# A head in written order on all engines, product stores on the SP queue, later block loads

## The chip, the cores and the metric

The kernel runs on one core of one Trainium2 chip. The metric is the device time of one launch in microseconds (us).

## The reference

Eight batches of 576 tokens, eight heads of 64. The computation is in float32:

```
scores = q k^T / 8;  ret = scores * D     # D[h,i,j] = gamma_h^(i-j) for i >= j, else 0
x  = (ret v)   as [4608 tokens, 512]
h  = ((x w1) * (x w2)) w3                 # w1, w2: 512 x 1024, w3: 1024 x 1024
y  = h w_out                              # 1024 x 512
u  = y w2_in                              # 512 x 2048
out = (u - tanh(u)) w2_out                # 2048 x 512
```

The weights come in as float64.

## The kernel before, in words

**Precision.** Each large product is made of three matmuls (`mm3`, lines 116 to 121: high x high, low x high, high x low). A float64 block of a weight ("raw", 512 KB) is turned into a high and a low part by a `Conv` job (lines 123 to 169): `load` is a DMA on the SP queue, `a` and `c` are one ACT instruction each (lines 141, 158), `b` is four DVE instructions (lines 146 to 149), `d` two (lines 164, 165). A `Queue` runs a job in two steps: step one is `b` of this job and the load of a later one, step two is `a` of the next job and `c`, `d`, `e` of this one.

**Attention.** A batch is five chunks of 128 tokens (the last has 64), 40 chunks in all. For each chunk: `attn_load` (three DMAs on SP, line 223; scaling of q on DVE, line 227, and of v by eight ACT instructions, line 215), `attn_1` (transposes of q and k on PE, line 238, copied out by ACT, line 242), `attn_2` (scores on PE, line 255, masked by two DVE instructions into `pt`, line 257), `attn_3` (product with the running state, line 353, with v, line 359, the update of the state, lines 367 to 377, and the result split into the high and low part of the token tile `x`, ACT line 384 and DVE line 385). Batches 0 and 1 (chunks 0 to 9, the "head") go this way. From chunk 10 on, "the third batch" and those behind it, q and k come in small block loads instead (`load_qk`, 32 DMAs per pair of chunks, put in the list `pend` and issued on SP by `trickle`, line 291, at most ten per unit), k and v by `load_kv` (line 307), POOL scales q (`stage_q`) and DVE transposes both (`stage_0`, lines 338 and 340).

**Units.** 12 token tiles of 384 by 8 column blocks are 96 units. A unit is two halves (`half_s`, 12 matmuls each, line 119 to 121, into PSUM tile `psab`), then ACT copies the first half out (`a`, line 412) and DVE multiplies it with the second (`pf`, line 417). The product goes to DRAM (`pdr`), from where the next stage loads it (`p_load`, line 646). Its store is issued on the ACT queue in the unit behind (list `late`, line 415). Tile `tp` has two buffers.

**Order.** In the prologue and in units 0 to 9 only PE's order is the written one (`manual_schedule(engines={PE})`, line 512); the other engines and queues are ordered by the planner. From unit 10 (`NAUTO`, line 554) all engines follow the written order. `conv_at` (line 545) says how many steps of the w1/w2 conversion stand in front of unit n; `chunk_at` says at which unit a chunk's `attn_3` stands. From unit 16 `side_s` runs the conversions of w_out and w3 (95 steps over the remaining units), the product w3 w_out, and at the end those of half of w2_out. A stage of chunk i has its unit in `stages` (line 550). A DMA handed to `later` is issued by `tick` some units on.

Of the kernel before, what the change touches and what calls it, by code (L numbers as in the profile page):

```python
# [8 lines left out]
F32 = mybir.dt.float32  # L9
# [19 lines left out]
def retention_glu_tanh_kernel(  # L29
# [16 lines left out]
    PE, ACT, DVE, POOL, SP = nc.tensor, nc.scalar, nc.vector, nc.gpsimd, nc.sync  # L46
# [3 lines left out]
    P = 128  # L50
# [3 lines left out]
    CH = [(s, min(C, S - s)) for s in range(0, S, C)]  # L54
    NA = len(CH)
    KD = DM // P
    FF = w1.shape[1] // P
    FF2 = w2_in.shape[1] // P
    T = 384
# [9 lines left out]
    pdr = [dram.tile([P, FF, T], F32, name=f"pdr{i}") for i in range(NTL)]  # L69
# [20 lines left out]

    sl_ = ExitStack()
    xp = sl_.enter_context(tc.tile_pool(name="xp", bufs=3, reuse_waits="tile"))
    tp = sl_.enter_context(tc.tile_pool(name="tp", bufs=2, reuse_waits="tile"))
# [9 lines left out]
    def later(eng, o, i_, n):  # L105

        held.append([n, eng, o, i_])

    def tick():
        for e in held:  # L110
            e[0] -= 1
        while held and held[0][0] <= 0:
            _, eng, o, i_ = held.pop(0)
            eng.dma_start(out=o, in_=i_)
# [88 lines left out]
    A = {}  # L203
# [13 lines left out]
    def attn_load(i):  # L217
        b, c = chunks[i]
        s0, n = CH[c]
        ts = []  # L220
        for nm, src in zip("qkv", qsrc):
            t = sap.tile([P, H, D], F32, name=f"{nm}n", bufs=4)
            SP.dma_start(out=t[:n], in_=src[b, s0:s0 + n])
            ts.append(t)
        A[i] = ts
        qn, kn, vn = ts
        DVE.tensor_tensor(qn[:n], qn[:n], dec_q[:n, c, :].unsqueeze(2).to_broadcast([n, H, D]), op=ALU.mult)
        scale_act(vn, dec_v, n, c)

    def attn_1(i):  # L230
        b, c = chunks[i]
        s0, n = CH[c]
        qn, kn, vn = A[i]
        tr = []
        for nm, src in (("q", qn), ("k", kn)):
            ps = psa.tile([P, NP, C], F32, tag="a", name=f"ps{nm}")
            for j in range(NP):
                PE.transpose(
                    ps[:, j, :n], src[:n, 2 * j:2 * j + 2, :].rearrange("p h d -> p (h d)"), ident[:n, :n]
                )  # L240
            t = sap.tile([P, NP, C], F32, name=f"{nm}T")
            ACT.activation(t[:, :, :n], ps[:, :, :n], AF.Copy)
            tr.append(t)
        A[i] = (kn, vn, tr[0], tr[1])
# [100 lines left out]
    def attn_3(i):  # L345
        b, c = chunks[i]
        s0, n = CH[c]
        kn, vn, qT, pt = A.pop(i)
        po = psa.tile([P, NP, C], F32, tag="a", name="pso")
        if c > 0:  # L350
            for j in range(NP):
                for e in range(2):
                    PE.matmul(  # L353
                        po[D * e:D * e + D, j, :n], state[:, j, D * e:D * e + D], qT[:, j, :n],
                        start=(j == 0), stop=False, skip_group_check=True,
                    )
        for j in range(NP):
            for e in range(2):
                PE.matmul(  # L359
                    po[D * e:D * e + D, j, :n], vn[:n, 2 * j + e, :], pt[:n, j, e, :n],  # L360
                    start=(c == 0 and j == 0), stop=(j == NP - 1), skip_group_check=True,
                )
        if c + 1 < NA:
            pu = psa.tile([P, NP, D], F32, tag="a", name="psu")
            for j in range(NP):
                for e in range(2):
                    PE.matmul(
                        pu[D * e:D * e + D, j, :], kn[:n, 2 * j + e, :], vn[:n, 2 * j + e, :],
                        start=True, stop=True,
                    )  # L370
            for e in range(2):
                sl = slice(D * e, D * e + D)
                st = state[sl, :, sl]
                if c == 0:
                    DVE.tensor_copy(st, pu[sl])
                else:
                    DVE.tensor_tensor(st, pu[sl], st, op=ALU.add)
        t0 = b * S + s0
        while t0 < b * S + s0 + n:
            ti = t0 // T  # L380
            m = min((ti + 1) * T, b * S + s0 + n) - t0
            x = xtile(ti)
            a0, o0 = t0 - b * S - s0, t0 - ti * T
            ACT.activation(x[:, 0, :, o0:o0 + m], po[:, :, a0:a0 + m], AF.Copy)
            DVE.tensor_tensor(  # L385
                x[:, 1, :, o0:o0 + m], po[:, :, a0:a0 + m], x[:, 0, :, o0:o0 + m].bitcast(F32), op=ALU.subtract
            )
            t0 += m


    ws = {}
    late = []

    def half_s(t, m, i):
        x = xt[t]
        w = ws[m]
        ps = psm.tile([P, 512], F32, tag="m", name="psab")
        for kk in range(KD):
            o = i * 1024 + kk * P
            mm3(  # L400
                ps[:, :T], (w[:, o:o + P], w[:, o + 512:o + 512 + P]), (x[:, 0, kk, :], x[:, 1, kk, :]),
                kk == 0, kk == KD - 1,
            )
        return ps

    def unit_s(t, m, mid=None):
        pss = [half_s(t, m, 0)]
        if mid is not None:
            mid()
        pss.append(half_s(t, m, 1))  # L410
        a = tp.tile([P, T], F32, name="a")
        ACT.activation(a, pss[0][:, :T], AF.Copy)  # L412
        while late:
            o, i_ = late.pop()
            ACT.dma_start(out=o, in_=i_)
        pf = tp.tile([P, T], F32, name="pf")
        DVE.tensor_tensor(pf, a, pss[1][:, :T], op=ALU.mult)  # L417
        late.append((pdr[t][:, m], pf))
        if m == FF - 1:
            del xt[t]  # L420

# [86 lines left out]
            yield  # L508


    ordered = ExitStack()
    ordered.enter_context(tc.manual_schedule(engines={mybir.EngineType.PE}))
    NH = 2 * NA
    for c in range(3):
        attn_load(c)
        q12.jobs[c].load()
    attn_load(3)
    attn_1(0)
    attn_1(1)
    attn_2(0, sap)  # L520
    q12.step()
    q12.step()
    attn_3(0)
    attn_load(4)
    attn_2(1, sap)
    attn_1(2)
    q12.step()
    attn_3(1)
    attn_load(5)
    attn_2(2, sap)  # L530
    attn_1(3)
    q12.step()
    attn_3(2)
    attn_load(6)
    attn_2(3, sap)


    units = [
        (0, 0), (0, 1), (0, 2), (0, 3), (0, 4), (1, 0), (1, 1), (1, 2),
# [2 lines left out]
    N0 = len(units)  # L542
    units += [(t, m) for t in range(2, NTL) for m in range(FF)]

    conv_at = [5, 9, 13, 17, 20, 21, 22, 23, 25, 27, 29, 31, 32]

    chunk_at = {0: 2, 1: 3, 2: 4, 3: 5, 4: 6, 6: 7, 8: 8, 10: 9}
    stages = []
    for i in range(NH, len(chunks)):
        p = int(13.0 + 2.3 * (i - NH))  # L550
        stages += [(p - 1, stage_q, (i,)), (p, stage_0, (i,)), (p + 1, stage_1, (i,)), (p + 2, attn_3, (i,))]
    stages.sort(key=lambda e: e[0])

    NAUTO = 10
    TRK = 10
    SIDE = 95
    sn = 0
# [3 lines left out]
    w34_ = ExitStack()  # L561
    w34 = []
    for n, (t, m) in enumerate(units):
        if n == NAUTO:
            ordered.close()
            ctx.enter_context(tc.manual_schedule())
        if n < len(conv_at):
            while q12.n < conv_at[n]:
                q12.step()
        if n == N0:  # L570
            assert not q12.step()
            sa_.close()
            cv = cv_.enter_context(tc.tile_pool(name="conv", bufs=2, side="right", reuse_waits="tile"))
            wg = wg_.enter_context(tc.tile_pool(name="wg", bufs=2, side="right", reuse_waits="tile"))
            for f in range(FF):
                wo[f] = wg.tile([P, 1024], F32R, name=f"wo{f}", bufs=1)
            side = side_s()
        while side is not None and sn < (n - N0 + 1) * SIDE / (len(units) - N0 - 1):
            sn += 1
            if next(side, 1) == 1:  # L580
                side = None
        tick()
        trickle(TRK)
        i = chunk_at.get(n)
        if i is not None and i > 2:
            attn_3(i)
            if i + 4 < NH:
                attn_load(i + 4)
            if i + 1 < NH:
                attn_2(i + 1, sap)  # L590
        unit_s(t, m, (lambda: attn_1(i + 2)) if i is not None and i + 2 < NH else None)
        if n == 5:
            load_qk(NH)
            load_kv(NH)
        if n == 8:
            load_qk(next_pair(NH))
        while si < len(stages) and stages[si][0] <= n:
            stages[si][1](*stages[si][2])
            si += 1
    assert si == len(stages) and not pend and not held and len(w34) == FF, (si, len(pend), held)  # L600
    assert side is None or next(side, None) is None
    for o, i_ in late:
        ACT.dma_start(out=o, in_=i_)
    sl_.close()
    lp_.close()

# [244 lines left out]
```

## Time and profile before

| | |
|---|---|
| runs, median of 3 | 1669.49 us (1668.22 to 1792.84) |
| the profiled execution's own time | 1668.11 us |
| its span | 1666.3 us |
| PE busy | 1607.6 us, 96% |
| DVE, ACT, POOL busy | 67%, 53%, 2% |
| mean granted clock of TensorE | 0.992 of 2.4 GHz |

The span runs from the first to the last instruction; 1.8 us of the execution's own time lie outside it. Busy shares are means over stages with different limits: in the first two of the page's 40 slices PE is busy for 5 tenths, in nearly all others for 9 tenths or more. "SPq" and "ACTq" in a row are DMA issues on those queues; a matmul's row shows a span that overlaps with the next one's, so the pace of matmuls is read from one start to the next.

### The profile page before, as it was taken

The page shows a single profiled execution, that of the slowest core. Times are in us where ns is not written, and L with a number is a line of the kernel's source. Part 1 is how long each engine was busy: PE and PEld are TensorE (multiplying, and loading weights), DVE is VectorE, ACT ScalarE, POOL GpSimd, SP SyncE. Part 2 cuts the span into 40 slices and gives each one's busy share as a digit, 9 for nine tenths or more (in the row PEclk, how much of TensorE's full clock was granted, in tenths as well). Part 3 has the DMA queues.
Part 4 walks back from the last instruction along what each step waited for, and adds up shares of the span by engine and source line. Part 5 has one row for each costly group of instructions (what it writes and reads, how often), then busy time and mean ns, then how long its engine had stood idle before and what let it go on. Part 6 is the DMA issues. An engine that isn't in the chain of part 4 may idle for free.

```text
span 1666.3 us, 26840 instructions
## 1 busy us (share of the span) xinstructions
PE 1607.6 (96%) x10128; PEld 1492.9 (90%) x10128; DVE 1118.6 (67%) x2006; ACT 876.4 (53%) x1929; POOL 31.1 (2%) x35
## 2 busy tenths in 40 slices
PE   5599989999999999999999999999999999999999
PEld 4489979989899999999999999999999999999997
DVE  6484655545454455676758788787887887778776
ACT  5352333323233232444447777777777777777775
POOL 0000000000001000000000000000000000000000
PEclk9799999999999999999999999999999999999999
DMA  8831565555546465766641001000100010001000
GB/s 195 193 105 66 132 149 131 143 126 141 114 117 141 109 254 191 218 203 221 198 188 45 20 20 38 20 20 19 39 19 20 20 38 20 20 19 39 1 19 20
DMA packets 261250, 157.96 MB, mean 95 GB/s; under 512 B 209152, under 2 KB 238080, under 8 KB 261120
## 3 DMA queue, kind: packets, MB, share of 16 engines
q1 hardware_dynamic: 245568, 127.93, 28.6%
q10 hardware_dynamic: 15552, 28.32, 4.5%
q8 instruction: 79, 1.29, 0.3%
q14 instruction: 51, 0.42, 0.1%
HBM read 110.05 MB, written 46.14 MB: 94 GB/s over the span
## 4 chain that ended last, share of the span: by engine, by line
PE 88%; SPq 4%; DMA 3%; DVE 2%; ACT 1%; issue 1%; ACTq 0%; DVEq 0%
PE psh L121 8%; PE psh L119 8%; PE psh L120 8%; PE psout L121 8%; PE psout L119 8%; PE psout L120 8%; PE psab L119 7%; PE psab L121 7%; PE psab L120 7%; PE psy L121 4%; PE psy L119 4%; PE psy L120 4%; SPq L291 3%; PE pss L255 2%; PE pso L359 1%; PE pso L353 1%
## 5 line engine op out<-in xcount | busy, mean ns | idle before, releaser
L119 PE MATMUL psab<-x,w 128*128 128x384 f32 x768 | 266.0, 346 | 0.0
L121 PE MATMUL psab<-x,w 128*128 128x384 f32 x768 | 259.0, 337 | 1.2 <-DVE x L385 1.2
L121 PE MATMUL psh<-yhl,w2i 128*128 128x384 f32 x768 | 258.9, 337 | 0.0
L120 PE MATMUL psab<-x,w 128*128 128x384 f32 x768 | 258.6, 337 | 0.0
L119 PE MATMUL psh<-yhl,w2i 128*128 128x384 f32 x768 | 258.1, 336 | 0.0
L120 PE MATMUL psh<-yhl,w2i 128*128 128x384 f32 x768 | 257.9, 336 | 0.0
L121 PE MATMUL psout<-w2o,g 128*128 128x512 f32 x576 | 227.0, 394 | 0.0
L119 PE MATMUL psout<-w2o,g 128*128 128x512 f32 x576 | 226.8, 394 | 0.0
L120 PE MATMUL psout<-w2o,g 128*128 128x512 f32 x576 | 225.4, 391 | 0.0
L740 ACT ACTIVATE u<-psh 128x384 f32<-128x384 f32 x192 | 94.4, 492 | 222.3 <-PE psh L121 222.1
L748 DVE TENSOR_TENSOR w<-u,psh 128x384 f32<-128x384 f32 x192 | 106.0, 552 | 80.7 <-ACT th L742 80.5
L761 DVE TENSOR_TENSOR g<-w,g 128x384 fp32r<-128x384 f32 x192 | 107.0, 557 | 69.9 <-ACT g L760 69.8
L120 PEld LDWEIGHTS psh<-yhl,w2i 128*128 128x128 f32 x768 | 144.2, 188 | 8.5
L119 PEld LDWEIGHTS psh<-yhl,w2i 128*128 128x128 f32 x768 | 144.3, 188 | 8.1
L119 PEld LDWEIGHTS psab<-x,w 128*128 128x128 f32 x768 | 145.7, 190 | 5.1
L417 DVE TENSOR_TENSOR pf<-a,psab 128x384 f32<-128x384 f32 x96 | 53.0, 552 | 140.4 <-PE psab L121 89.6
L121 PEld LDWEIGHTS psab<-x,w 128*128 128x128 f32 x768 | 145.3, 189 | 1.5 <-DVE x L385 1.5
L120 PEld LDWEIGHTS psab<-x,w 128*128 128x128 f32 x768 | 145.8, 190 | 0.5
L121 PEld LDWEIGHTS psh<-yhl,w2i 128*128 128x128 f32 x768 | 144.2, 188 | 0.0
L121 PEld LDWEIGHTS psout<-w2o,g 128*128 128x128 f32 x576 | 108.1, 188 | 25.6
L412 ACT ACTIVATE a<-psab 128x384 f32<-128x384 f32 x96 | 46.9, 488 | 159.4 <-PE psab L121 141.0
L119 PE MATMUL psy<-p,w 128*128 128x384 f32 x384 | 128.4, 334 | 1.9 <-ACT p L651 1.9
(85 smaller groups left out, 2901.5 us busy)
## 6 DMA issues: line engine op xcount, KB each, us to landing
pdr<-pf ACTq DMA_DIRECT2D x96, 192.0 KB, 2.3
pin<-pdr SPq DMA_DIRECT2D x48, 384.0 KB, 4.1
raw<-in_moe_w_dram SPq DMA_DIRECT2D x32, 512.0 KB, 5.4
raw<-in_moe_w_out_dram SPq DMA_DIRECT2D x24, 512.0 KB, 4.1
ydr<-ys ACTq DMA_DIRECT2D x12, 768.0 KB, 5.7
yin<-ydr SPq DMA_DIRECT2D x12, 768.0 KB, 4.2
out_dram<-os SPq DMA_DIRECT2D x36, 256.0 KB, 2.3
kn<-in_k_dram SPq DMA_DIRECT2D x32, 256.0 KB, 3.3
```

What stands on the lines that cost most here:

```text
L119: PE.matmul(ps, lh, rh, start=first, stop=False)
L120: PE.matmul(ps, ll, rh, start=False, stop=False)
L121: PE.matmul(ps, lh, rl, start=False, stop=last)
L255: PE.matmul(pss[e][:n, j, :n], kT[r:r + D, j, :n], qT[r:r + D, j, :n], start=True, stop=True)
L291: SP.dma_start(out=o, in_=i_)
L353: PE.matmul(po[D * e:D * e + D, j, :n], state[:, j, D * e:D * e + D], qT[:, j, :n], start=(j == 0), stop=False, skip_group_check=True,)
L359: PE.matmul(po[D * e:D * e + D, j, :n], vn[:n, 2 * j + e, :], pt[:n, j, e, :n], start=(c == 0 and j == 0), stop=(j == NP - 1), skip_group_ ...
L412: ACT.activation(a, pss[0][:, :T], AF.Copy)
L417: DVE.tensor_tensor(pf, a, pss[1][:, :T], op=ALU.mult)
L740: ACT.activation(u, h, AF.Square)
L748: DVE.tensor_tensor(w, u, h, op=ALU.mult)
L761: DVE.tensor_tensor(g[:, 1, :], w, g[:, 0, :].bitcast(F32), op=ALU.subtract)
```

## The change

All engines follow the written order from the beginning. In the prologue and in units 0 to 10 the instructions are written in a new order: loads of chunks 0 and 1 ahead of the first weight block, the scalings of q and v apart from the loads (`attn_scale`), the split into x apart from the rest of `attn_3` (`attn_x`), each ahead of the conversion steps that stand beside it. In a unit, `finish` (the copy `a`, the product `pf`) now stands behind the first half of the unit after; its store goes to the SP queue by `later(SP, ..., 1)`, issued at the start of the unit after that, ahead of the block loads of that unit; `pf` has three buffers. The conversion steps stand between the halves of the unit before the one that needs them. The first block loads of the third batch are put in the list after units 10 and 13 (before: 5 and 8), and the stages of its chunks start one unit later. After the last unit `finish` and `tick` issue the last two stores on SP.

```diff
+    ctx.enter_context(tc.manual_schedule())
...
+    def attn_scale(i):
...
+    def attn_x(i):
...
-    def unit_s(t, m, mid=None):
-        pss = [half_s(t, m, 0)]
-        if mid is not None:
-            mid()
-        pss.append(half_s(t, m, 1))
+    def finish():
+
+        if not open_:
+            return
+        t, m, pss = open_.pop()
         a = tp.tile([P, T], F32, name="a")
         ACT.activation(a, pss[0][:, :T], AF.Copy)
-        while late:
-            o, i_ = late.pop()
-            ACT.dma_start(out=o, in_=i_)
-        pf = tp.tile([P, T], F32, name="pf")
+        pf = tp.tile([P, T], F32, name="pf", bufs=3)
         DVE.tensor_tensor(pf, a, pss[1][:, :T], op=ALU.mult)
-        late.append((pdr[t][:, m], pf))
+        later(SP, pdr[t][:, m], pf, 1)
...
-    for c in range(3):
-        attn_load(c)
-        q12.jobs[c].load()
+    attn_load(0)
+    attn_load(1)
+    q12.jobs[0].load()
+    attn_load(2)
+    q12.jobs[1].load()
     attn_load(3)
+    q12.jobs[2].load()
+    attn_scale(0)
     attn_1(0)
+    attn_scale(1)
+    attn_2(0, sap)
     attn_1(1)
-    attn_2(0, sap)
     q12.step()
-    q12.step()
+    attn_scale(2)
     attn_3(0)
+    attn_x(0)
     attn_load(4)
     attn_2(1, sap)
+    q12.step()
     attn_1(2)
-    q12.step()
     attn_3(1)
     attn_load(5)
+    q12.step()
     attn_2(2, sap)
+    attn_x(1)
+    attn_scale(3)
     attn_1(3)
     q12.step()
     attn_3(2)
+    attn_x(2)
     attn_load(6)
     attn_2(3, sap)
+    attn_scale(4)
...
-    conv_at = [5, 9, 13, 17, 20, 21, 22, 23, 25, 27, 29, 31, 32]
+    conv_at = [8, 12, 16, 20, 21, 22, 23, 25, 27, 29, 31, 32]
...
-        p = int(13.0 + 2.3 * (i - NH))
+        p = int(14.0 + 2.28 * (i - NH))
...
-        unit_s(t, m, (lambda: attn_1(i + 2)) if i is not None and i + 2 < NH else None)
-        if n == 5:
+            if i + 2 < NH:
+                attn_scale(i + 2)
+        want = conv_at[n] if n < len(conv_at) else 0
+        pss = [half_s(t, m, 0)]
+        finish()
+        if want:
+            while q12.n < (want + q12.n) // 2:
+                q12.step()
+        if i is not None and i + 2 < NH:
+            attn_1(i + 2)
+        while q12.n < want:
+            q12.step()
+        pss.append(half_s(t, m, 1))
+        open_.append((t, m, pss))
+        if n == 10:
             load_qk(NH)
             load_kv(NH)
-        if n == 8:
+        if n == 13:
             load_qk(next_pair(NH))
...
-    for o, i_ in late:
-        ACT.dma_start(out=o, in_=i_)
+    finish()
+    tick()
```

## Rows read from the trace of the kernel before

**Rows 1.** Busy time by stage: window, length, each engine's busy time, clock, DMA share

```profile
0.00:110.00 110.00, 69.85 (x700) 62.10 (x701) 70.62 (x133) 52.65 (x141) 4.86 (x9) 0.92 0.80 183
...
200.00:240.00 40.00, 33.31 (x250) 31.04 (x250) 24.96 (x45) 13.77 (x41) 4.93 (x4) 0.91 0.59 138
240.00:560.00 320.00, 314.58 (x2567) 292.07 (x2566) 161.36 (x292) 97.06 (x271) 20.66 (x21) 0.99 0.53 129
```

**Rows 2.** PE's waits from 0 to 110: what waited for what: total, times, longest

```profile
PE psk L238 <- DVE x L385: 15.4, 2, 14.6
```

**Rows 3.** Timeline of DVE and ACT: start, length, instruction, idle time before

```profile
49.82 0.55 DVE L417 TENSOR_TENSOR pf<-a,psab 128x384 f32<-128x384 f32 x1
...
66.92 0.34 ACTq L415 DMA_DIRECT2D pdr<-pf  x1
67.31 0.60 ACT L384 ACTIVATE x<-pso 128x512 fp32r<-128x512 f32 x1 [18.34 <-DMA qb<-in_q_dram]
```

**Rows 4.** Chain that ended last, from 0 to 260: start, length, step

```profile
62.65 4.20 DMA qb<-in_q_dram
```

**Rows 5.** Timeline of SP, its first and last run of early block loads

```profile
23.92 3.68 SPq L291 DMA_DIRECT2D qb<-in_q_dram  x4
...
76.87 2.59 SPq L291 DMA_DIRECT2D kb<-in_k_dram  x5
```

**Rows 6.** Start of the head: busy time by window, then DVE's first instruction

```profile
0.00:20.00 20.00, 7.40 (x42) 6.11 (x44) 8.57 (x15) 11.20 (x32) 0.73 (x5) 1.00 1.02 224
...
5.26 0.69 DVE L227 TENSOR_TENSOR qn<-qn,dec 128x512 f32<-128x512 f32 x1 [5.26 <-DMA qn<-in_q_dram]
```

**Rows 7.** Timeline of PE: transposes; unit 5; attn_3 of chunk 7; unit 6

```profile
87.19 0.63 PE L238 MATMUL psq<-cst,qn 128*128 128x128 f32 x4
...
101.50 0.33 PE L119 MATMUL psab<-x,w 128*128 128x384 f32 x1
...
105.76 1.09 PE L353 MATMUL pso<-qT,state 128*64 128x128 f32 x16
...
109.21 0.44 PE L119 MATMUL psab<-x,w 128*128 128x384 f32 x1
```

**Rows 8.** Timeline of DVE: attention, then one conversion job

```profile
108.79 0.85 DVE L377 TENSOR_TENSOR state<-psu,state 64x256 f32<-64x256 f32 x2
...
111.47 1.28 DVE L257 TENSOR_TENSOR pt<-pss,cst 128x512 f32<-128x512 f32 x2
112.67 0.42 DVE L148 TENSOR_SCALAR ct<-cf 128x512 uint32<-128x512 uint32 x1
...
115.06 0.42 DVE L146 TENSOR_SCALAR ct<-raw 128x512 uint32<-128x512 uint32 x1
```

**Rows 9.** PE's waits from 110 to 700, the longest

```profile
PE pso L359 <- ACT vn L215: 6.3, 1, 6.3
```

**Rows 10.** Timeline ahead of that wait: SP's weight loads, and ACT behind them

```profile
206.87 0.39 SPq L135 DMA_DIRECT2D raw<-in_moe_w_out_dram  x1
...
219.38 0.38 SPq L135 DMA_DIRECT2D raw<-in_moe_w_out_dram  x1
...
223.49 0.66 ACT L141 ACTIVATE cf<-raw 128x512 f32<-128x512 f32 x1 [10.88 <-DMA raw<-in_moe_w_out_dram]
```

**Rows 11.** Timeline of SP: runs of block loads at a quick and a slow pace

```profile
162.27 4.59 SPq L291 DMA_DIRECT2D qb<-in_q_dram  x10
...
244.24 7.70 SPq L291 DMA_DIRECT2D kb<-in_k_dram  x14
```

**Rows 12.** Chain that ended last, from 600 to 660: from unit 95 to the stage behind

```profile
658.53 0.56 DVE pf L417
659.12 0.33 ACTq L603
659.49 0.85 ACT p L651
```

**Rows 13.** Loads of products (tile pin), all of the run: issue to landing

```profile
DMA to landing us min/median/max: 3.0/4.1/6.5
```

More of the change, by code (lines that the diff above doesn't have):

```diff
@@ L225, in attn_load @@
         A[i] = ts
-        qn, kn, vn = ts
+    def attn_scale(i):
+        b, c = chunks[i]
+        s0, n = CH[c]
+        qn, kn, vn = A[i]
         DVE.tensor_tensor(qn[:n], qn[:n], dec_q[:n, c, :].unsqueeze(2).to_broadcast([n, H, D]), op=ALU.mult)
@@ L377, in attn_3 @@
                     DVE.tensor_tensor(st, pu[sl], st, op=ALU.add)
+        A[i] = po
+    def attn_x(i):
+        b, c = chunks[i]
+        s0, n = CH[c]
+        po = A.pop(i)
         t0 = b * S + s0
@@ L391, in retention_glu_tanh_kernel @@
     ws = {}
-    late = []
+    open_ = []
     def half_s(t, m, i):
@@ L508, in side_s @@
             yield
-    ordered = ExitStack()
-    ordered.enter_context(tc.manual_schedule(engines={mybir.EngineType.PE}))
     NH = 2 * NA
-    for c in range(3):
-        attn_load(c)
-        q12.jobs[c].load()
+    attn_load(0)
[3 more added lines that the diff above has]
+    q12.jobs[1].load()
     attn_load(3)
+    q12.jobs[2].load()
+    attn_scale(0)
     attn_1(0)
+    attn_scale(1)
+    attn_2(0, sap)
     attn_1(1)
-    attn_2(0, sap)
     q12.step()
-    q12.step()
+    attn_scale(2)
     attn_3(0)
+    attn_x(0)
     attn_load(4)
     attn_2(1, sap)
+    q12.step()
     attn_1(2)
-    q12.step()
     attn_3(1)
     attn_load(5)
+    q12.step()
     attn_2(2, sap)
+    attn_x(1)
+    attn_scale(3)
     attn_1(3)
@@ L533, in retention_glu_tanh_kernel, with attn_4 @@
     attn_3(2)
+    attn_x(2)
     attn_load(6)
     attn_2(3, sap)
+    attn_scale(4)
+    def attn_4(i):
+        attn_3(i)
+        attn_x(i)
     units = [
@@ L549, in retention_glu_tanh_kernel @@
     for i in range(NH, len(chunks)):
-        p = int(13.0 + 2.3 * (i - NH))
-        stages += [(p - 1, stage_q, (i,)), (p, stage_0, (i,)), (p + 1, stage_1, (i,)), (p + 2, attn_3, (i,))]
+        p = int(14.0 + 2.28 * (i - NH))
+        stages += [(p - 1, stage_q, (i,)), (p, stage_0, (i,)), (p + 1, stage_1, (i,)), (p + 2, attn_4, (i,))]
     stages.sort(key=lambda e: e[0])
-    NAUTO = 10
     TRK = 10
@@ L563, in retention_glu_tanh_kernel @@
     for n, (t, m) in enumerate(units):
[L564 to L569, printed above, removed]
         if n == N0:
@@ L586, in retention_glu_tanh_kernel @@
             attn_3(i)
+            attn_x(i)
             if i + 4 < NH:
@@ L599, in retention_glu_tanh_kernel @@
             si += 1
-    assert si == len(stages) and not pend and not held and len(w34) == FF, (si, len(pend), held)
+    assert si == len(stages) and not pend and len(held) < 2 and len(w34) == FF, (si, len(pend), held)
     assert side is None or next(side, None) is None
-    for o, i_ in late:
-        ACT.dma_start(out=o, in_=i_)
+    finish()
+    tick()
     sl_.close()
```

## The prediction

> **What bounds the kernel now.** I read the page's 40 slices first: PE is nearly full everywhere except in the first two, so PE's idle time is the quantity to follow. The table of windows then sizes it [rows 1]: in the first 110 us PE is busy for 69.85, so 40.2 us are idle; 6.7 more are idle from 200 to 240, 5.4 from 240 to 560; all the rest of the run has some 6. The span is 1666.3 us and PE is busy for 1607.6, so only what happens to these 58.7 us of idle time (and the work done at a low clock around them) can pay. Next, the view of PE's waits: one wait makes 14.6 of the 40.2 [rows 2]. Its cause is in the timelines: `pf` of unit 0 is done at 50.4, its store leaves the ACT queue at 66.92, and the split of `x` right behind it on ACT had been idle for 18.34 us [rows 3]. The releaser is a block load that SP issued at 62.65 and that took 4.20 us [rows 4]: the store on ACT stood until a load for the third batch had landed, which SP had not even issued when `pf` was ready. SP was so late because all 64 early block loads (16 runs, 23.92 to 79.5) were mixed in between the loads of the head [rows 5].
>
> **The change, part by part.**
>
> *Stores off ACT, block loads late.* With the store on SP nothing on ACT waits for DMAs in front of `x`; the 14.6 us wait loses its cause. The 64 block loads, about 0.46 us of SP each [rows 11], or 29 us, leave the head's stretch. What is late next is DVE.
>
> *The head in written order.* I follow the written queues by hand. Loads: the first 20 us moved 224 GB/s with the DMA engines full [rows 6]; a chunk is 0.786 MB, a weight block 0.524 MB, so in the new order chunk 0 is there at about 6, chunk 1 at 9.5, block 0 at 12, chunk 2 at 15.3, block 1 at 17.6, chunk 3 at 21. DVE's first work is at 5.26 as before. On ACT the eight scalings of v now stand ahead of the copies of the transposes, so `kT` of chunk 0 is ready at 9.3, the masks of chunk 0 end at 12.7, `x` of chunk 0 at 18.4, the state of chunk 1 at 22.9, the masks of chunk 2 at 26.2, q of chunk 3 at 27.4, and `x` of chunk 2, with which token tile 0 is whole, at 33.1. PE's longest gap in this is 4.3 us (transposes of chunk 3, behind one conversion step, the masks and the `x` of DVE). Unit 0 starts its third matmul at 33.1, and DVE begins the conversions of unit 1 at 34.9.
> Units 0 to 3 each need two conversion jobs beside a chunk. A job on DVE is 2.39 us for four instructions, from 112.67 to 115.06 [rows 8], 0.42 and 0.69 for the other two: 3.3 to 3.5. A chunk is 0.69 (q), 1.2 (masks), 0.85 (state), 0.69 (`x`), and the unit 0.55 (`pf`) [rows 3, 6, 8]. Together 10.6 at most. PE needs 4.26 for 24 matmuls (101.50 to 105.76), 3.45 for scores, outputs and state, 1.2 for transposes [rows 7]: 8.9. So DVE sets the pace here: 6.6, 9.7, 9.3 and 10.3 us for units 0 to 3 (chunk 4 is half a chunk), and the conversions of unit 3 end at 70.7. PE, two halves and one chunk behind, ends unit 4 at 77.5. Before, unit 5 began at 101.50 [rows 7] with the same work behind it: 24 us less. My hand count has no time for signals between engines and for late loads; some 25 hops of 0.1 us and 1 to 2 us of loads in the prologue make 4. **Head: 20 us less.** Bounds: 8 (the engines block each other in the fixed order as much again as they did) and 25.
>
> *Adds a wait: the store on SP* stands until `pf` is done, in the middle of the unit before its own place. Behind it on SP are chunk loads and weight blocks in the head, block loads later. In the head SP waits longer for a free buffer anyway (block 8 may go at 46.7, when `pf` of unit 0 is done at 44.6): nothing.
>
> *From unit 11 to unit 27* the list of block loads never runs dry: 17 units of ten. SP: 170 loads at the quick pace of 0.46 are 78 us; some eight runs behind a weight block go at the slow pace, 14 in 7.70 instead of 6.4 [rows 11], 10 us; 16 k and v loads at 0.5 are 8, 8 weight blocks at 0.39 [rows 10] are 3; 17 stores at 0.4, taken like the weight blocks' issues, 7: 106 us. PE: 17 units of 4.26 and seven chunks of 3.45 [rows 7] are 97. SP falls 9 us behind. In the kernel before the same list is full from unit 16 on, and there it made the 6.3 us wait [rows 9]: SP issued two weight blocks 12.5 us apart, ACT idled 10.88 us for the second, the scaling of v stood behind it [rows 10]. This wait stays in the new kernel: the 95 steps of the conversions are still spread over 79 units, so that units 20 and 25 get two steps, the load of a block and its first use; and the copy `a` now stands behind those steps, so ACT has one unit less of slack. I take 2 us at unit 16, 2 at unit 20 and 6 at unit 25, against 6.7: **3 us more.** Bounds: 8 less (no wait left, and the work at a low clock beside it, granted 0.91 in that window [rows 1], regained) and 11 more.
> The Trainium skill, DMA: Bandwidth & Descriptors, section Issuing engines are not separate DMA queues, says that DMAs run on the same 16 DMA engines whoever starts them, and that the choice of the engine saves issue time only, usually small beside the transfer. By that rule the stores' 7 us on SP would count as nothing, and the sum would be 1653. The rows speak against the second half: ten issues in a row took SP 4.59 us [rows 11], more than a unit's matmuls.
>
> *From unit 28 to 82* SP needs per unit 8.4 block loads (96 in 11.4 units) at 0.47, 0.45 for k and v (two per 2.28 units at 0.5), 0.3 for weights, 0.4 for the store: 5.1 us, against 320/54 = 5.9 us of a unit [rows 1]: hidden. If the cover goes, see the second rival.
>
> *After unit 95* the last store stands on SP ahead of the first weight block and the first product loads of the next stage; in the kernel before the store was on ACT, and the split of the first loaded product followed it at once, so the loads were done [rows 12]. `pf` ends at 659.1 [rows 12]. Store 0.35, weight block 0.4, then the load, landing in 3.0 to 4.1 [rows 13], then the split on ACT, 0.85 [rows 12]: PE goes on at 664 to 665 instead of 660.3. **4 us more, 5 with a low clock after the wait.** Bounds 3 and 7.
>
> *One answer each:* POOL's scaling and the stages a unit later end at unit 82 of 96, hidden; `pf` with three buffers only takes a wait away; from 662 on nothing is changed.
>
> Sum against the profiled execution's own 1668.1 (1.4 below the median of the runs): 1668.1 - 20 + 3 + 5 = **1656 us**.
>
> **The rivals.** *Stores and block loads find room (chance 0.18):* head 24 to 25 less, unit 16 to 27 without a wait, 8 less, end 4 more: 1640. For it: SP's early share is moved to units 11 to 15; before, SP took up the list again only at 162.27 [rows 11]. Against: the list is then full for 17 units without a rest.
> *SP becomes the bound of the batches (0.13):* the place is units 28 to 82, the price the pace of the block loads. At 0.47 SP has 0.8 us to spare per unit; at 0.55, the slow run of rows 11, 0.1; at 0.60 a unit would be 6.2 us on SP, 0.3 too long, 16 us over 54 units: 1668 - 20 + 5 + 11 + 16 = 1680 with the middle at its upper bound, slower than before. It decides from 0.56 on. Against: in the trace SP also waits there for its buffers.
> *The written order blocks (0.17):* DVE, ACT and PE wait in turn, so the head keeps 30 of its 40 us of idle time: 8 less, 1668.
> *The stall is not undone (0.07):* the store takes the same wait to the SP queue, and the chunk loads behind it come as late as `x` did: head as before, 1673.
>
> **How the numbers follow.** Forecast 0.45, the rivals 0.18, 0.13, 0.17, 0.07. The forecast's own bounds, head 25 to 12 with the middle 0 to 8, are 1648 to 1669. The range 1641 to 1672 takes in that, half of the first rival, the third and part of the fourth; out are the second and half of the first, about 0.2 in all. Two per cent, about what a measurement of this kernel can tell from no change, is 33 us: 1636 to 1703. Below lies the far end of the first rival, 0.05; above the far end of the second, 0.03; within, 0.92.
>
> **What would show it.** In the profile after: no DMA issue on ACT in the head; no wait of PE over 5 us before 80; PE idle about 20 us up to unit 5, which begins near 82; DVE nearly full from 35 to 70; the block loads' first issue after 105; a wait of PE of 2 to 8 us between 130 and 210 with ACT's `cf` waiting for a weight block; PE idle some 6 us between the last `psab` and the first `psy`, with the store on SP just ahead of the product loads. I am wrong if PE's idle time in the head stays over 30 us, or if waits for `kT`, `qT` or `qb` (block loads too late) show from 240 to 560.

## The result, and the profile after

The changed kernel takes 1687.12 us (median of 4 runs, 1683.68 to 1687.88), the kernel before 1669.12 (median of 4 runs): 1.0106 times as long, interval 1.0086 to 1.0126. One slow run of the kernel before, of 1792.84 us, is left out of the ratio. The changed kernel is 18 us slower, where 13 us less were forecast, and lies above the range of 1641 to 1672. The profiled execution took 1687.88 us, with a span of 1686.1, 19.8 more than before.

The windows of the kernel after show where (window, length, busy time of PE, PE's weight loads, DVE, ACT, POOL, then granted clock, DMA share, GB/s); they answer to [rows 1]:

```profile
0.00:110.00 110.00, 83.96 (x831) 77.00 (x832) 77.64 (x141) 54.21 (x147) 0.73 (x5) 0.94 0.68 156
110.00:240.00 130.00, 109.43 (x845) 104.69 (x844) 67.85 (x123) 36.09 (x101) 9.34 (x9) 0.91 0.54 128
240.00:560.00 320.00, 310.83 (x2516) 289.16 (x2514) 158.60 (x291) 90.86 (x271) 19.27 (x20) 0.99 0.52 125
560.00:680.00 120.00, 109.20 (x763) 104.64 (x760) 54.15 (x98) 30.05 (x73) 0.62 (x1) 0.96 0.52 175
```

The kernel before, in the same two later windows:

```profile
110.00:240.00 130.00, 123.31 (x998) 117.09 (x997) 76.27 (x138) 40.84 (x109) 5.56 (x5) 0.97 0.40 103
...
560.00:680.00 120.00, 117.68 (x794) 114.79 (x793) 65.09 (x112) 37.01 (x81) 0.00 (x0) 1.00 0.59 202
```

PE's idle time is the window's length less its busy time. It falls by 14.1 us up to 110 (40.2 to 26.0), and rises by 13.9 from 110 to 240 (6.7 to 20.6), by 3.8 from 240 to 560 and by 8.5 from 560 to 680. That is 12 us more (11.5 over the whole span). The other 8.4 us are busy time: the page has PE busy for 1616.0 us instead of 1607.6 with the same 10128 matmuls. More of them ran at the lower clock behind waits: 0.91 was granted from 110 to 240 and 0.96 from 560 to 680, before 0.97 and 1.00.

PE's waits after, in the two stretches (what waited for what: total, times, longest). The first fence is 0 to 110, the second everything from 110 on:

```profile
PE psq L243 <- DVE qn L232: 19.9, 7, 5.9
PE pss L260 <- ACT kT L247: 4.0, 1, 4.0
PE psq L243 <- DVE state L380: 2.0, 1, 2.0
```

```profile
PE psab L120 <- ACT a L423: 26.9, 6, 10.6
PE psy L120 <- ACT p L679: 7.1, 1, 7.1
PE pst L464 <- DVE w3f L163: 6.5, 3, 3.4
```

The 14.6 us wait of [rows 2] is gone and DVE's pace is what is left of the head, as forecast. What is new is the copy `a`: six times PE waited for the PSUM tile that it frees. The timeline of ACT has the reason, at the three longest of them:

```profile
154.30 0.68 ACT L142 ACTIVATE cf<-raw 128x512 f32<-128x512 f32 x1 [15.80 <-DMA raw<-in_moe_w_out_dram]
154.88 0.48 ACT L423 ACTIVATE a<-psab 128x384 f32<-128x384 f32 x1
...
183.40 0.66 ACT L142 ACTIVATE cf<-raw 128x512 f32<-128x512 f32 x1 [10.15 <-DMA raw<-in_moe_w_out_dram]
...
222.59 0.66 ACT L142 ACTIVATE cf<-raw 128x512 f32<-128x512 f32 x1 [12.90 <-DMA raw<-in_moe_w_out_dram]
```

Each time ACT stands at a conversion whose weight block has not landed, and `a` is behind it. And the block is late because SP comes to it late. SP's timeline ahead of the last one:

```profile
202.09 0.40 SPq L136 DMA_DIRECT2D raw<-in_moe_w_out_dram  x1
202.58 1.66 SPq L115 DMA_DIRECT2D pdr<-pf  x1
204.29 4.92 SPq L296 DMA_DIRECT2D kb<-in_k_dram  x10
209.31 0.39 SPq L115 DMA_DIRECT2D pdr<-pf  x1
209.75 0.97 SPq L296 DMA_DIRECT2D kb<-in_k_dram  x2
210.81 3.85 SPq L296 DMA_DIRECT2D qb<-in_q_dram  x8
214.71 0.45 SPq L312 DMA_DIRECT2D kn<-in_k_dram  x1
215.27 0.52 SPq L312 DMA_DIRECT2D vn<-in_v_dram  x1
215.88 0.85 SPq L136 DMA_DIRECT2D raw<-in_moe_w_out_dram  x1
216.82 0.38 SPq L115 DMA_DIRECT2D pdr<-pf  x1
217.26 6.07 SPq L296 DMA_DIRECT2D qb<-in_q_dram  x8
```

Read it as a list with hardly a hole: two weight blocks are 13.8 us apart (12.5 in [rows 10]), and in between SP issues one DMA after another, two stores among them. Its one long stand is the first store, 1.66 us instead of 0.4, which waited for `pf`.

### The profile page after: what moved, and what is told of

Same layout as the page of the kernel before. It is cut to its first block, busy times and chain, and to the rows that moved or that the text cites. A ratio compares the mean times of both kernels' runs of the same rounds, so it can differ in the third digit from the quotient of the medians.

```text
span 1686.1 us, 26796 instructions
## 1 busy us (share of the span) xinstructions
PE 1616.0 (96%) x10128; PEld 1502.7 (89%) x10128; DVE 1118.5 (66%) x2006; ACT 868.4 (52%) x1929; POOL 30.0 (2%) x35
## 4 chain that ended last, share of the span: by engine, by line
PE 84%; SPq 5%; DVE 5%; DMA 4%; issue 1%; ACT 1%; DVEq 0%; ACTq 0%
PE psh L122 8%; PE psh L120 8%; PE psh L121 8%; PE psout L122 8%; PE psout L120 8%; PE psout L121 8%; PE psab L120 6%; PE psab L122 5%; PE psab L121 5%; PE psy L120 4%; PE psy L122 4%; PE psy L121 4%; SPq L296 4%; DMA raw<-in_moe_w_out_dram 2%; PE pss L260 1%; PE pso L364 1%
## 5 line engine op out<-in xcount | busy, mean ns | idle before, releaser
L120 PE MATMUL psab<-x,w 128*128 128x384 f32 x768 | 269.4, 351 | 26.9 <-ACT a L423 26.9
L122 PE MATMUL psab<-x,w 128*128 128x384 f32 x768 | 262.0, 341 | 0.0
L121 PE MATMUL psab<-x,w 128*128 128x384 f32 x768 | 261.8, 341 | 0.0
L120 PEld LDWEIGHTS psab<-x,w 128*128 128x128 f32 x768 | 148.1, 193 | 32.7 <-ACT a L423 28.1
L121 PEld LDWEIGHTS psab<-x,w 128*128 128x128 f32 x768 | 148.3, 193 | 0.4
L122 PEld LDWEIGHTS psab<-x,w 128*128 128x128 f32 x768 | 147.9, 193 | 0.4 <-DVE x L396 0.4
L120 PE MATMUL psy<-p,w 128*128 128x384 f32 x384 | 129.4, 337 | 7.1 <-ACT p L679 7.1
L122 PE MATMUL psy<-p,w 128*128 128x384 f32 x384 | 129.3, 337 | 0.0
L121 PE MATMUL psy<-p,w 128*128 128x384 f32 x384 | 129.2, 336 | 0.0
```

Source lines behind the costliest of these rows:

```text
L120: PE.matmul(ps, lh, rh, start=first, stop=False)
L121: PE.matmul(ps, ll, rh, start=False, stop=False)
L122: PE.matmul(ps, lh, rl, start=False, stop=last)
```

## The experiments

Ratios are to the kernel before, run on the same chip beside each; the changed kernel has 1.0106. "After" and "before" in a heading say which kernel was edited.

### 1. After, copy and product first

```diff
+        if n > N0:
+            finish(2)
         while side is not None and sn < ...
...
-        finish()
+        if n <= N0:
+            finish()
...
```

The store keeps its place in SP's list (it is handed over earlier and held one unit longer, in lines not shown).

> From unit 17 on the copy `a` and the product `pf` of a unit stand ahead of the next unit's conversion steps again, as in the kernel before; all else as changed. Order theory (the copy stands on ACT behind a conversion that waits for a late weight block, and PE waits for the PSUM tile that the copy frees): the six waits of PE for `a`, 26.9 us in all, fall to under 8, and the time to about 1666, as the low clock behind these waits goes too. Queue theory (SP, with the stores and a list of block loads that never runs dry, delivers weight blocks too late, whatever stands behind them on ACT): other waits of the same size take their place, on the scaled v or on pt, and the time stays above 1680.

1681.06 us, ratio 1.0060 (1.0043 to 1.0076), 6 us less than the changed kernel. PE's waits for `a` fell from 26.9 us to 5.3, but 13.7 us of waits of the scores for `qT` came up in their place. The block is still late; the order theory alone fails.

### 2. After, stores on ACT

```diff
-        later(SP, pdr[t][:, m], pf, 1)
+        later(ACT, pdr[t][:, m], pf, 1)
```

> The changed kernel with the product stores issued on the ACT queue instead of SP, at the same place in the written order. Queue theory: SP gets 96 issues of about 0.4 us back, some 0.6 us per unit with its waits, the weight blocks come earlier and PE's waits for `a` fall from 26.9 to under 12; time about 1672. Order theory: the weight blocks still come behind the ten block loads of a unit, the waits fall by 3 to 6 us only; time 1680 to 1684. If the store's wait for a landing blocks ACT again as in the kernel before, a wait of over 5 us comes back in the head.

1667.36 us, ratio 0.9983 (0.9973 to 0.9992): 20 us from one word. PE's waits from 110 on:

```profile
PE psab L120 <- ACT a L423: 15.4, 6, 7.1
PE pst L464 <- DVE w3f L163: 6.0, 3, 2.8
PE psy L120 <- ACT p L679: 2.0, 1, 2.0
```

The wait for `a` is down by 11.5 us, not quite to the 12 expected, and the one at the end by 5.1 (the loads of the next stage no longer stand behind the last store). From 110 to 240 it is 11.2 us, in the changed kernel 20.6. The weight blocks did not land faster: from 110 to 260 they took 4.6 us from issue to landing (median) in both kernels, so it is their issue that came earlier. No wait over 5.7 us is in the head: in this order the stores on ACT do not block it.

### 3. After, block loads early

```diff
-        if n == 10:
+        if n == 5:
             load_qk(NH)
...
-        if n == 13:
+        if n == 8:
```

> The changed kernel with the first block loads of the third batch put in the list after units 5 and 8 again (before's places); the stages stay one unit late. Queue theory: SP has its 64 block loads behind it by unit 12 and some 15 us of rest ahead of unit 16, so the first waits for `a` (6.1 us near 150, 3.8 near 185) vanish and the later ones shrink; time about 1674. Order theory: only the wait at unit 16 goes, 6 us, time about 1680. The head may lose up to 3 us to the added traffic.

1682.86 us, ratio 1.0074 (1.0059 to 1.0089), 4 us less; waits for `a` 22.9 instead of 26.9. Between the two theories. The interval just touches that of the changed kernel, so the later list is a small part at most.

### 4. After, last store on ACT

```diff
+    tick()
     finish()
-    tick()
+    while held:
+        _, _, o, i_ = held.pop()
+        ACT.dma_start(out=o, in_=i_)
```

> The changed kernel with only the very last product store issued on ACT, so that the first weight block and product loads of the next stage don't stand behind it on SP. Both theories on the middle say nothing here. By the prediction's step on the end, PE's wait for the first split product, 7.1 us, falls to about 1.9 as before, and the time by 5 to 6 us, to about 1681.

PE's wait for the first split product fell from 7.1 to 2.8. The time, 1684.71 us, ratio 1.0076 (1.0056 to 1.0096), overlaps with that of the changed kernel: the wait's cause is shown, its 4 to 5 us in the total are not told from noise here.

### 5 and 6. After, stores on SP at other places

```diff
-        later(SP, pdr[t][:, m], pf, 1)
+        later(SP, pdr[t][:, m], pf, 2)
...
```

> The changed kernel, stores still on SP, but issued one unit later again (age 2 instead of 1); same number of issues, same three buffers of `pf`. The store on ACT took 20 us off, which leaves two readings. Wait theory (SP stands at the store until `pf` is done, and the block loads and the weight block written behind it start that much later; 19.9 us of such waits from 100 to 260): the waits of SP for `pf` fall under 5 us there and the time to 1668 to 1674. Issue theory (96 issues of 0.4 us are too many for a full queue): SP's waits go but the time stays above 1682. If instead `pf` then waits for its own buffer, DVE shows waits for pdr and the time stays too.

```diff
+        trickle(TRK)
         tick()
-        trickle(TRK)
```

> The changed kernel with the store of a unit written behind that unit's ten block loads on SP instead of ahead of them. Same issues. Wait theory: the ten loads no longer stand behind `pf`, half a unit to a unit of run-ahead is won; time 1670 to 1678. Issue theory: above 1682.

1682.79 us, ratio 1.0081 (1.0060 to 1.0102), and 1687.39 us, ratio 1.0110 (1.0095 to 1.0125). SP's waits for `pf` from 100 to 600 fell from 39.6 us to 12.7 and 17.5, and the time by 4, which noise can make (the intervals overlap), and by nothing; PE still waited 23.6 and 27.9 us for `a`. The wait that the store brings is a small part at most.

### 7 and 8. After, stores on ACT and copy first; the same with block loads early

These join the edits of runs 1 and 2, and of 1, 2 and 3.

> Stores on ACT (which gave 1667) and, from unit 17, the copy and the product ahead of the conversion steps again. What is left of PE's waits for `a` with the stores on ACT is 15.4 us in six. Order theory for this rest: they go, 1655 to 1659. If the late weight block only moves the wait on (to the scaled v, qT or pt, as with the stores on SP, where it won 6 us of 27): 1661 to 1666.

> As the run before it in this group, and the first block loads of the third batch after units 5 and 8 again. If SP's list that never runs dry from unit 11 to 27 makes the rest of the late weight blocks, 4 to 8 us less than that run, about 1652; if not, the same within 2 us.

1661.59 us, ratio 0.9950 (0.9933 to 0.9967): the copy's place is worth 6 us once more, as in run 1. What is left is moved on in part: 12.0 us of waits for `qT`, one of 9.7 at unit 25. 1662.52 us, ratio 0.9958 (0.9943 to 0.9973): with the stores off SP the late list costs nothing that the runs can tell.

### 9. After, stores on ACT and one small load per unit on SP

```diff
         tick()
+        SP.dma_start(out=tiny, in_=consts[:, 0:4])
         trickle(TRK)
...
```

> Stores on ACT (1667 alone), and at the place where the changed kernel had a store SP issues a load of 2 KB (16 bytes on each partition) into a tile that nothing reads: one more issue per unit, no product behind it, no wait for `pf`. Issue theory (a place in SP's list and a landing to be waited for is what costs): the 12 to 15 us of the middle come back, 1677 to 1682. Payload or wait theory (192 KB on SP's queue, or the wait for `pf`): 1667 to 1670.

1678.43 us, ratio 1.0054 (1.0039 to 1.0070), 11 us more than run 2, 0.0071 in ratio. PE's first wait from 110 on:

```profile
PE psab L120 <- ACT a L424: 26.0, 7, 9.9
```

The sum is the 26.9 of the changed kernel again, with 2 KB instead of 192 KB and without a wait for `pf`, but it lies elsewhere. First from 110 to 240 (run 2 has 11.2, the changed kernel 20.6), then from 240 to 560 (1.6 and 2.6), where SP also stood for the landing of its own small load of the unit before, as the last line has it:

```profile
PE psab L120 <- ACT a L424: 13.7, 2, 9.9
```

```profile
PE psab L120 <- ACT a L424: 7.2, 3, 6.3
...
SPq L598 <- DMA tiny<-in_consts_dram: 18.8, 8, 3.3
```

So a place more per unit in SP's list is enough to cost 11 us, with next to nothing moved. But the loss from 110 to 240 comes back only in part (2.5 of 9.4 us), and behind 240 the place and the wait that it brought cannot be told apart. That the issue alone made the changed kernel's loss is not shown by this run.

### 10. After, as run 7 with weight blocks two jobs ahead

```diff
-            self.pool, bufs = (hv, 4) if self.pool == "head" else (cv, 2)
+            self.pool, bufs = (hv, 4) if self.pool == "head" else (cv, 3)
...
-            self.t = self.pool.tile([P, 512], F32, name="ct")
+            self.t = self.pool.tile([P, 512], F32, name="ct", bufs=1)
...
-        pf = tp.tile([P, T], F32, name="pf", bufs=3)
+        pf = tp.tile([P, T], F32, name="pf")
...
-        qu = Queue(jobs)
+        qu = Queue(jobs, ahead=2)
```

> Stores on ACT, copy and product first (1661.6), and the weight blocks of the side work loaded two jobs ahead instead of one (three raw buffers; room for them from one ct and one pf buffer less). If late weight blocks make what is left of PE's waits from 110 to 560 (12.0 us for qT, behind the conversions on DVE, and 7.9 for w3f): these fall to under 6 us together, 1645 to 1650. If SP's list makes block loads of q and k late instead: no gain, 1660 or more.

1653.52 us, ratio 0.9902 (0.9882 to 0.9922). The waits for `qT` fell from 12.0 to 2.1 us, those for `w3f` stayed (8.5); at least 3 us less was won than expected. From 110 to 240 PE is busy for 126.71 of 130 us, in the changed kernel for 109.43: the late weight blocks were what was left of the waits there.

### 11 and 12. Before, with one part of the change each

Run 11 has the copy behind the conversion steps from unit 16 on (first part of the diff), run 12 the stores on SP from unit 10 on (the rest; `eng_` begins as ACT):

```diff
         pss = [half_s(t, m, 0)]
+        finish()
...
             o, i_ = late.pop()
-            ACT.dma_start(out=o, in_=i_)
+            eng_[0].dma_start(out=o, in_=i_)
...
             ordered.close()
+            eng_[0] = SP
```

> The kernel before with one part of the change: from unit 16 on, the copy `a` and the product of a unit stand behind the first half of the unit after, so behind its conversion steps. Its own late weight block at unit 25 (6.3 us) then blocks PE sooner, through `a`. Order theory: 4 to 8 us slower than before, 1674 to 1677. If the place of the copy matters only together with a crowded SP: within 2 us of before.

> The kernel before with one part of the change: from unit 10 on the product stores (not the last) are issued on SP, behind the block loads of the unit. Queue theory: 8 to 15 us slower, 1677 to 1685, with waits of PE behind late weight blocks from 160 to 560. If stores on SP are harmful only with the copy behind the conversion steps or the late list: within 4 us of before.

1675.36 us, ratio 1.0037 (1.0024 to 1.0050), with 13.1 us of waits for `a` that the kernel before did not have (its 6.3 us for `vn` have gone); and 1677.60 us, ratio 1.0043 (1.0027 to 1.0060). Each edit alone slows the old kernel, by 6 and 8 us. The 8 are not the stores' alone, though: in run 12 the planner also issued 14 of the 64 early block loads behind the head, from 127 to 135, and the expected waits behind weight blocks hardly show. PE idles for 7.4 us from 110 to 240, before 6.7; the larger part of the loss is 5.3 us more of busy time.

### 13. After, as run 10 with attention first in the prologue

```diff
-    q12.step()
     attn_2(2, sap)
     attn_x(1)
     attn_scale(3)
     attn_1(3)
     q12.step()
+    q12.step()
```

> The fastest so far (1653.5: stores on ACT, copy first, weight blocks two ahead) with the third conversion step of the prologue written behind the scaling and the transposes of chunk 3. In the changed kernel PE waits 4.8 us for that scaling at 31.5, and the granted clock is 0.66 from 21 to 36. If this gap and the low clock behind it are what the head fell short by (14 us gained where 20 were forecast): PE idle up to 110 falls by 2 to 4 us and the time to 1647 to 1650. If DVE's pace sets the head anyway, what is gained early is lost by unit 3: 1652 to 1654.

1646.79 us, ratio 0.9852 (0.9836 to 0.9869), 24 us faster than before, outside run 10's interval. The stretch from 21 to 36 of the changed kernel, and of this run:

```profile
21.00:36.00 15.00, 10.13 (x106) 9.36 (x106) 8.53 (x16) 5.82 (x15) 0.00 (x0) 0.66 0.88 188
```

```profile
21.00:36.00 15.00, 11.46 (x156) 9.96 (x154) 13.01 (x24) 8.95 (x25) 0.00 (x0) 1.00 1.15 238
```

In 15 us PE starts 156 matmuls instead of 106, and the granted clock is 1.00 instead of 0.66. Run 10, of which this is an edit, has 114 and 0.79 there: 1.00 up to the gap, 0.50 behind it from 31.4 to 36. (In the changed kernel the clock had dipped once ahead of the gap too, 0.65 from 21 to 24.)

### 14. Before, block loads late

```diff
-        if n == 5:
+        if n == 10:
...
-        if n == 8:
+        if n == 13:
...
-        p = int(13.0 + 2.3 * (i - NH))
+        p = int(14.0 + 2.28 * (i - NH))
```

> The kernel before, planner in the head and stores on ACT, with only the block loads of the third batch put in the list after units 10 and 13 and its stages later as in the change. My reading of the head (a store on ACT stands until an early block load has landed, and `x` behind it): the 18.3 us wait on ACT and the 14.6 us wait of PE go, the middle loses some 4 us to the later list; 1655 to 1662. If the planner's own order of the head was the cause: the wait stays or another of over 8 us takes its place, 1668 or more.

1678.30 us, ratio 1.0044 (1.0029 to 1.0059). The planner put 50 of the 64 loads into the head again, the first at 23.45, and ACT's wait stayed:

```profile
ACT x L384 <- DMA qb<-in_q_dram: 18.6, 1, 18.6
```

So it does not test the head. It shows that the rest of the edit, 14 later loads and the stages a unit later, costs the middle 7 us: 13.4 us of waits of the scores for `qT`.

### 15. Before, the head's stores on SP

Run 12's edit turned round: SP up to unit 9, ACT from unit 10.

> The kernel before with the product stores of units 0 to 9 on SP (the planner orders them there), from unit 10 on ACT as before. My reading of the head (ACT stands at a store until an early block load lands): ACT's 18.3 us wait in front of `x` goes, PE's wait of 14.6 falls under 4, time 1655 to 1660. If the loads themselves, on a slow SP queue, made the head late: PE waits for q, k or converted weights instead, at least 8 us in one place, and the time stays above 1664.

1659.37 us, ratio 0.9936 (0.9921 to 0.9950). PE's waits up to 110 begin with

```profile
PE psq L238 <- DVE qn L227: 10.5, 2, 6.1
PE pss L255 <- ACT kT L242: 4.0, 3, 1.7
```

The wait for `x` has gone from 15.4 to 1.1 us. The store on ACT was the cause, with the block loads still in place.

### 16. After, as run 13 with block loads early

> The fastest (1646.8) with the first block loads of the third batch after units 5 and 8 again, as in the kernel before. What is left from 110 to 560 is 9.2 us of idle time, most of it on w3f. If SP's list still costs there: 1643 to 1645. If the blocks are in time already: within 2 us of 1646.8; if they delay the head's weight blocks: above 1649.

1646.06 us, ratio 0.9864 (0.9848 to 0.9880), the same as run 13. Either one is some 1.4% faster than the kernel before.

## Why the prediction was wrong

**The stall in the head: right, and shown.** Run 15 takes the store off ACT in the head and edits nothing else, and 11 us go. In the changed kernel no wait of PE before 80 is longer than 5.9 us, and that one is for the first load.

**The head, 20 us less forecast, 14.5 measured.** Unit 5 began at 101.50 [rows 7]; in the changed kernel, by the timeline of PE, units 0 and 5 begin at

```profile
37.84 0.44 PE L120 MATMUL psab<-x,w 128*128 128x384 f32 x1
...
87.01 0.34 PE L120 MATMUL psab<-x,w 128*128 128x384 f32 x1
```

The hand count had 77.5, and 82 with its 4 us of slack. It found the longest gap in its place (4.3 us, measured 4.8, in front of chunk 3's transposes) but ran all that came behind at full speed. Nearly all of the 5 us is lost ahead of unit 0, which begins at 37.84, where the count had its third matmul at 33.1. In run 13, with this gap shortened and the clock up, units 0 and 5 begin at 32.68 and 81.59: gap and clock are what the step missed. (Its 10.6 us at most for DVE take a job at 3.3 us; at 3.5 they are 11.0.) 14.5 is inside its bounds.

**The middle, 3 us more forecast, at most 11: the step that failed.** By PE's idle time from 110 to 560 it is 17.7 us, and more with the low clock. The prediction named the mechanism, SP's list too long by 9 us, the weight block late, `a` behind the conversion. Its sum had SP 106 us of list for PE's 97, and then it priced this as three waits of 2, 2 and 6 us against the 6.7 of before. They measured 6.1, 3.8 and 10.6: the list was right to be over, but only a third of its excess was charged to PE, and no low clock. What run 2 shows in its place, with the stores off SP, is 1.9, 2.2 and 7.1. The 9.4 us between the two are no less than the issue time of the 19 stores in this stretch (0.4 us each, 7.6 in all): what the list was over by was paid in full, not in part. Most of it is the issue and not the stand for `pf`: in run 5 this stand falls from 11.2 us to 2.4 there, and the waits for `a` only from 20.6 to 17.4 (one profile each). And the block's lateness was the mechanism: with the blocks two jobs ahead, in run 10, PE idles for 3.3 us there, in run 7 for 10.8. Behind each wait come matmuls at the lower clock (8.4 us of busy time more in the whole run).

In time, the order of the copy is worth 6 us, in runs 1, 7 and 11 alike; the stores 20, from the changed kernel to run 2 and from run 1 to run 7, some 5 of them at the end; the later list up to 4, in run 3, and nothing once the stores are off SP. That the list also stands in part while PE waits, since its buffers wait for the same units, is my reading; no run takes it apart. Neither sign of being wrong that the prediction names has shown (26.0 us idle in the head, no wait for `kT`, `qT` or `qb` from 240 to 560): the loss came where it had put a small one.

**The rule of the Trainium skill** (DMA: Bandwidth & Descriptors, Issuing engines are not separate DMA queues) that the choice of the issuing engine saves little but issue time is borne out as far as the transfer goes: weight blocks landed in 4.6 us with and without the stores on SP. That the issue time is usually small beside the transfer holds for one store (0.4 us to issue, 2.4 to landing, medians of the 19), but does not help here. Issues add up on their queue, and their sum decided this stretch.

**From unit 28 to 82: nearly hidden,** 3.8 us more of idle time from 240 to 560. The second rival had the right queue and the right side, but put the loss into this stretch and into the pace of the block loads; most of it came before 240.

**The end, 5 us more forecast.** PE's wait rose from 1.9 to 7.1 us, as computed; the store stood ahead of the loads, and run 2, with it on ACT, has 2.0 again. The psy matmuls behind it started 0.32 us apart up to 684, at a granted clock of 0.50, against 0.17 later. With another wait for `a` of 3.7 us near 610 the window lost 8.5.

**The chances:** faster, same and slower by 2% had 0.05, 0.92 and 0.03, and the 1.1% lies within; the sign was wrong. That 2% is about what a measurement can tell from no change was wrong too: the interval here is 0.4% wide. And the fourth rival's 1673 leaves out the middle's 3 us.

## What to carry to other kernels

When one queue issues nearly all DMAs, count its list per stage, in issues, before moving anything onto it; a queue that was over by a tenth here cost PE all of its excess, and moving 96 stores to a queue with room won 20 us. Ask of each copy that frees a PSUM tile what stands ahead of it in its engine's order: a conversion that waits for a load there turns a late load into a stall of PE. In a planned order, a store on a compute engine's queue can wait for a load that another queue has not yet issued (why the two were tied here is not shown); look for an idle engine whose releaser is a DMA that it does not use.

## What was not expected

A load of 2 KB, with nothing behind it, cost 11 us over the run, where stores of 192 KB cost 20 (runs 9 and 2). Whether it is its issue or the wait for its landing that costs is open: in that run the small load took 3.8 us from issue to landing (median of the 18 between 110 and 240), a block load of 32 KB 2.1. And a gap of 4.8 us early in the head slowed what followed: outputs and update of chunk 2 took 3.4 us from 33.33 on (granted clock 0.58 from 33.3 to 36), of chunk 3, from 43.36 on, 2.4 (1.00).
